# Routing chunks of nine and nine tiles, and the softplus per attention unit on GpSimd

## The chip, the cores and the metric

One core of a Trainium2 chip runs the whole program. The metric is the device time of one execution in microseconds. Engines are called by the profile's names: PE (matmul) with PEld (its weight load), DVE (VectorE), ACT (ScalarE), POOL (GpSimd) and SP (which issues most DMAs). Each engine works through its own list of instructions in the order in which they were emitted; where a source needs another engine's result it waits at the head of that list.

## The reference, cut to what matters

The program is a chain of three stages over 2304 tokens of width 512: a packed attention, a mixture of eight experts with two experts a token, and a SiLU layer.

```python
logits = x @ w_gate
noise_scale = np.log1p(np.exp(x @ w_noise))          # softplus
noisy_logits = logits + noise_scale * noise
top2 = np.argpartition(-noisy_logits, 2, axis=1)[:, :2]
...
for e in range(E):
    for k in range(2):
        mask = top2[:, k] == e
        h = np.maximum(x[mask] @ w1[e], 0.0)
        out[mask] += top2_w[mask, k, None] * (h @ w2[e])
```

The change touches the softplus and the sorting of tokens to experts.

## The kernel before, in words

**Attention.** The tokens are 18 tiles of 128 rows. Eight packing units (`packed`, one for a batch and half of the heads) make small packed keys and values; ten unpacking units (`unpacked`, numbered 0 to 9, of one or two tiles: 0 to 3 hold tiles 0 to 7, 4 holds tile 8, 5 to 8 hold tiles 9 to 16, 9 holds tile 17) turn them into the tokens' rows. A unit's DVE steps are L398 (maximum), L400 (subtract), L402 (sum), L403, L404 and L405 (scale), with ACT's exponential L401 between L400 and L402. PE then transposes (`a2p`, L410) and multiplies (`xp`, L419, once for each half `g` of the width); the 16 routing logits of a tile come out beside the row, are collected by DVE in `lg` (L423 for the first half, L421 for the second), ACT copies the row into `xr`, and SP writes it to `xs` in DRAM (L426). There are two `xr` buffers.

**Routing.** `route` runs on a chunk of tiles: before on tiles 0 to 10 (chunk 0, `EARLY` = 11) and on 11 to 17 (chunk 1). It makes softplus out of ACT's exponential and logarithm for large arguments and a polynomial for small ones (L437 to L449, thirteen DVE instructions), the noisy logits (L451, L452), the two best experts (L456, L458), ranks within each expert (`rk`, PE with L471 and L473), and by one-hot products (L486, L488, L493, then PE's `ip`, L500) the list of token rows for each expert, `idx0` after chunk 0 (L503: the first two tiles' worth of expert 0) and `idx` after chunk 1 (L513). `few` and L620 to L622 give the count that decides the branch to a general path, which isn't taken here.

**Expert 0 ahead of the branch.** With `idx0`, POOL gathers two tiles of rows by indirect DMA (L155), PE transposes them (L145, `tps`), and the first block of expert 0 runs (`expert_block`, L167 to L169 and L177 to L179). While it runs, chunk 1 is routed; with `idx` POOL gathers five more tiles, which PE transposes between the block's last matmuls. PE's last transposes end this part, then all engines branch to `routed`, which holds the rest of the program.

**Order.** The units and routing steps are emitted by a slot loop: `START1` and `START2` give each unit's first slot, `LAG1` and `LAG2` its later phases; from slot 9 on, three steps of `route` for chunk 0 are emitted a slot (`RSTEP`). The framework then sets each engine's list by its own estimate of times. POOL also holds eight weight splits (`split`, L112, tensors `wa0l` to `wa7l`) and the copies into `ppBD` (L355) behind each packing unit's `px` (L350).

Of the kernel before, what the change touches and what calls it, by code (L numbers as in the profile page):

```python
# [7 lines left out]
F32 = mybir.dt.float32  # L8
# [11 lines left out]
P = 128  # L20
B, H, S, D, PK = 4, 8, 576, 64, 32
N, DM, E, F, FF = 2304, 512, 8, 1024, 2048
# [8 lines left out]
START2 = (3, 4, 5, 5, 6, 6, 8, 11, 12, 12)  # L31
SWITCH = 12
WLOAD = 4
RSTEP = 3
LAG2 = (0, 1, 3, 3)
BLOCKS = [(0, 2), (2, 4), (6, 4), (10, 4), (14, 4)]
BW = 512
TA, TB = 2, 3
EARLY = 11
LAG = 1  # L40
DELAY = 2

# [2 lines left out]
def body(ctx: ExitStack, tc: tile.TileContext, q, k, v, p, wg, wn, noise, w1, w2, w_in, w_out, out):  # L45
# [171 lines left out]
    with ExitStack() as ax:  # L217
# [147 lines left out]
            cp(A, bd[:, 256:272], wp)  # L365
            yield

        def unpacked(t, n, lg):

            pr, r = divmod(t, 9)  # L370
            qT = sb.tile([P, 8, P], F32, name="qT")
# [42 lines left out]
            for i in range(n):  # L414
                xr = sb.tile([P, 2, 256], F32, name="xr")
                for g in range(2):
                    xp = pMx.tile([P, 272], F32, name="xp", tag="m")
                    for b, sl in parts:
                        T.matmul(xp[sl], aT[:, 2 * i + g, sl], ppBD[b, g], start=True, stop=True)  # L419
                    if g:  # L420
                        V.tensor_tensor(lg[:, i, :], xp[:, 256:272], lg[:, i, :], op=OP.add)  # L421
                    else:
                        V.tensor_copy(lg[:, i, :], xp[:, 256:272])  # L423
                    cp(A, xr[:, g, :], xp[:, 0:256])
                r0 = (t + i) * P
                nc.sync.dma_start(xs[r0:r0 + P, :], xr.rearrange("p a b -> p (a b)"))  # L426
            yield

        def route(t0, n, lg):

            def tl(shape, nm, dt=F32):
                return rt.tile([P, n, *shape], dt, name=f"rt_{nm}{n}", tag=f"rt_{nm}", bufs=1)


            z = lg[:, :, 8:16]
            w, h, sp, sa, big = tl([E], "w"), tl([E], "h"), tl([E], "sp"), tl([E], "sa"), tl([E], "big", I32)
            V.tensor_tensor(w, z, z, op=OP.mult)  # L437
            V.tensor_scalar(sa, z, 20.0, None, op0=OP.min)
            A.activation(sa, sa, AF.Exp)
            A.activation(sa, sa, AF.Ln, bias=1.0)  # L440
            V.tensor_scalar(h, w, 31.0 / 14515200, -17.0 / 645120, op0=OP.mult, op1=OP.add)
            V.tensor_scalar(sp, z, 0.5, 0.6931471805599453, op0=OP.mult, op1=OP.add)
            V.tensor_tensor(h, h, w, op=OP.mult)
            V.tensor_scalar(big, w, 0.25, None, op0=OP.is_gt)
            for c in (1.0 / 2880, -1.0 / 192, 0.125):
                V.scalar_tensor_tensor(h, h, c, w, op0=OP.add, op1=OP.mult)
            V.tensor_tensor(sp, sp, h, op=OP.add)
            V.tensor_tensor(sa, sa, z, op=OP.max)
            V.copy_predicated(sp, big, sa)  # L449
            ny = tl([E], "ny")  # L450
            V.tensor_tensor(ny, sp, nzt[:, t0:t0 + n, :], op=OP.mult)  # L451
# [49 lines left out]
            if t0 + n < NT:  # L501
                V.tensor_tensor(idx_f, idx_f, ip, op=OP.add)
                V.tensor_scalar(idx0, idx_f[:, 0:TA], 0.0, float((t0 + n) * P - 1), op0=OP.max, op1=OP.min)  # L503
                sn = rt.tile([P, E], F32, name=f"sn{n}")
                V.tensor_reduce(sn, ob.rearrange("p n e -> p e n"), axis=AX.X, op=OP.add)
                V.tensor_tensor(seen, seen, sn, op=OP.add)
                V.tensor_copy(seen_b, seen)
                c = pMx.tile([P, E], F32, name="c", tag="m")
                T.matmul(c, ones, seen_b, start=True, stop=True)
                V.tensor_scalar(few, c, float(TA * P), float(N), op0=OP.is_lt, op1=OP.mult)  # L510
            else:
                V.tensor_tensor(idx_f, idx_f, ip, op=OP.add)
                V.tensor_scalar(idx, idx_f, 0.0, float(N - 1), op0=OP.max, op1=OP.min)  # L513
                sn = rt.tile([P, E], F32, name=f"sn{n}")
                V.tensor_reduce(sn, ob.rearrange("p n e -> p e n"), axis=AX.X, op=OP.add)
                V.tensor_tensor(seen_b, seen, sn, op=OP.add)
# [17 lines left out]

        chunks = {0: EARLY, EARLY: NT - EARLY}
        lgs = {t: one.tile([P, n, 16], F32, name=f"lg{t}") for t, n in chunks.items()}
        units1 = [(b, g) for b in range(B) for g in range(2)]
        units2 = [(0, 2), (2, 2), (4, 2), (6, 2), (8, 1), (9, 2), (11, 2), (13, 2), (15, 2), (17, 1)]
        run1, run2 = {}, {}
# [6 lines left out]
        def make2(i):  # L546
            t, n = units2[i]
            t0 = max(c for c in chunks if c <= t)
            return unpacked(t, n, lgs[t0][:, t - t0:t - t0 + n, :])

        def slot_steps(slot):
            for ph in (3, 2, 1, 0):
# [14 lines left out]
        for slot in range(START2[-1] + LAG2[-1] + 1):  # L567
# [23 lines left out]
            for i, s0 in enumerate(START1):  # L591
                if slot == s0 + WLOAD:
# [2 lines left out]
                        load_w1(W[0], 0, i, G)  # L595
                    else:
                        load_w2(W[0], 0, i - 4, G)
            if slot >= START2[5] + LAG2[3]:
                run(r0, RSTEP)
        for _ in r0:  # L600
            pass
        tick()
        tick()
        r1 = route(EARLY, NT - EARLY, lgs[EARLY])
# [297 lines left out]
```

## Time and profile before

| quantity | us |
|---|---|
| median of 3 runs | 1019.39 (1017.34 to 1020.85) |
| profiled execution, time | 1018.89 |
| profiled execution, span | 1016.9 |
| PE busy | 974.1 (96%) |
| DVE busy | 436.3 (43%) |
| ACT busy | 348.0 (34%) |
| POOL busy | 208.6 (21%) |

All times below are from the span's start. The profiled execution lies 0.5 us under the median. PE is busy for nearly all of the span; the stretch in which it isn't is the one before 161.55 us, where the routed part's first matmul stands.

### The profile page before, as it was taken

Reading aid. Unit: us, or ns where it says so; the run is one execution under the profiler, and the core shown is the slowest. Engines: PE = TensorE matmul, PEld = TensorE weight load, DVE = VectorE, ACT = ScalarE, POOL = GpSimd, SP = SyncE. Lnnn points to the kernel's source line nnn. Section 1 sums busy time; section 2 is a strip of 40 time slices with the busy share of each in tenths; the row PEclk is TensorE's granted clock in tenths of the full one; section 3 lists DMA queues with packets and bytes.
Section 4 is the critical chain, followed back from the end, with each engine's and each line's share of the span. In section 5 each row is a group of like instructions: output and inputs, shape, how many; then the busy total and the mean of one; then the engine's idle time right before and its main releaser. Section 6 shows DMA issues by size and latency. Waiting matters only on the chain.

```text
span 1016.9 us, 14321 instructions
## 1 busy us (share of the span) xinstructions
PE 974.1 (96%) x5672; PEld 836.5 (82%) x5672; DVE 436.3 (43%) x843; ACT 348.0 (34%) x631; POOL 208.6 (21%) x221
## 2 busy tenths in 40 slices
PE   6988796999999999999999998999999999999997
PEld 3776686899999989899999987888888888888885
DVE  3556762565656566575634356422212221111111
ACT  3575321443433334343423254222222222222221
POOL 2162011010101001010100116533323322222221
PEclk9988798999999999999999999999999999999999
DMA  9992224575766656575632436210111101001001
GB/s 247 242 279 90 81 65 137 169 245 147 239 180 210 199 186 219 175 223 181 217 105 93 138 124 204 73 42 22 42 42 32 32 14 39 1 1 42 1 0 42
DMA packets 80473, 122.48 MB, mean 120 GB/s; under 512 B 14608, under 2 KB 47376, under 8 KB 80400
## 3 DMA queue, kind: packets, MB, share of 16 engines
q1 hardware_dynamic: 74320, 101.57, 32.3%
q0 software_dynamic: 6080, 19.93, 6.5%
q8 instruction: 47, 0.77, 0.3%
q14 instruction: 26, 0.21, 0.1%
HBM read 93.17 MB, written 28.31 MB: 119 GB/s over the span
## 4 chain that ended last, share of the span: by engine, by line
PE 87%; DMA 4%; issue 3%; DVE 2%; SPq 2%; ACT 1%; POOL 1%; POOLq 0%; ACTq 0%; DVEq 0%
PE hps L167 13%; PE hps L169 13%; PE hps L168 13%; PE acc L178 13%; PE acc L177 13%; PE acc L179 13%; PE tps L145 2%; PE xp L419 2%; PE s L388 1%; DMA vm<-in_v_dram 1%; SPq L236 1%; DMA ys<-ysb 1%; DMA kr<-in_k_dram 1%; PE s L321 1%; DMA y<-ys,slots 1%
## 5 line engine op out<-in xcount | busy, mean ns | idle before, releaser
L702 POOL TENSOR_TENSOR gl<-sg,gh 128x512 fp32r<-128x512 f32 (+1 forms) x80 | 95.3, 1193 | 252.4 <-ACT gh L701 237.0
L190 ACT ACTIVATE hh<-hps 128x384 fp32r<-128x384 f32 (+1 forms) x128 | 56.1, 438 | 261.7 <-PE hps L169 249.6
L698 DVE TENSOR_TENSOR sg<-hps,sg 128x512 f32<-128x512 f32 (+1 forms) x80 | 50.7, 635 | 195.6 <-ACT sg L697 195.2
L191 DVE SCALAR_TENSOR_TENSOR hl<-hps,hh 128x384 fp32r<-128x384 f32 (+1 forms) x128 | 62.8, 490 | 149.5 <-ACT hh L190 147.5
L155 POOL DMA_INDIRECT xg<-xs,idx x40 | 42.9, 1072 | 355.2 <-PE tps L145 302.7
L697 ACT ACTIVATE sg<-hps 128x512 f32<-128x512 f32 (+1 forms) x80 | 44.4, 555 | 189.0 <-PE hps L169 186.0
L701 ACT ACTIVATE gh<-sg 128x512 fp32r<-128x512 f32 (+1 forms) x80 | 47.1, 589 | 82.3 <-DVE sg L698 82.1
L688 POOL DMA_INDIRECT y<-ys,slots x36 | 37.9, 1053 | 120.5 <-DMA ys<-ysb 82.9
L148 DVE TENSOR_TENSOR xla<-tps,xha 128x512 fp32r<-128x512 f32 x26 | 17.9, 690 | 30.0 <-ACT xha L147 29.9
L419 PE MATMUL xp<-ppBD,a2T 128*128 128x272 f32 (+1 forms) x80 | 26.4, 471 | 2.5 <-ACT xr L51 2.2
L148 DVE TENSOR_TENSOR xlb<-tps,xhb 128x512 fp32r<-128x512 f32 x32 | 22.0, 687 | 15.0 <-ACT xhb L147 14.9
L692 DVE SCALAR_TENSOR_TENSOR y<-y,gates,y 128x512 f32<-128x512 f32 x18 | 14.3, 796 | 28.9 <-DMA y<-ys,slots 28.8
L147 ACT ACTIVATE xhb<-tps 128x512 fp32r<-128x512 f32 x32 | 19.1, 597 | 19.1 <-PE tps L145 19.1
L691 DVE TENSOR_SCALAR y<-y,gates 128x512 f32<-128x512 f32 x18 | 9.2, 512 | 38.2 <-DMA y<-ys,slots 38.2
L167 PE MATMUL hps<-xhb,wa0h 128*128 128x384 f32 (+1 forms) x48 | 17.6, 367 | 7.8 <-issue 7.8
L145 PEld LDWEIGHTS tps<-ident,xg 128*128 128x128 f32 x160 | 19.7, 140 | 5.6 <-ACT xha L147 0.4
L145 PE MATMUL tps<-ident,xg 128*128 128x128 f32 x160 | 23.9, 272 | 0.2
L641 DVE SCALAR_TENSOR_TENSOR t<-raw,t 128x512 int32<-128x512 int32 x32 | 22.2, 693 | 1.1
L642 DVE SCALAR_TENSOR_TENSOR t<-raw,t 128x512 int32<-128x512 int32 x32 | 22.1, 690 | 0.9
L147 ACT ACTIVATE xha<-tps 128x512 fp32r<-128x512 f32 x26 | 15.5, 596 | 19.7 <-PE tps L145 19.7
L638 ACT ACTIVATE t<-raw 128x512 f32<-128x512 f32 x32 | 21.0, 658 | 0.0
L167 PE MATMUL hps<-xha,wa3h 128*128 128x256 f32 (+1 forms) x56 | 17.7, 316 | 3.2 <-DVE sg L698 3.2
(438 smaller groups left out, 2959.1 us busy)
## 6 DMA issues: line engine op xcount, KB each, us to landing
raw<-in_moe_w_dram SPq DMA_DIRECT2D x64, 512.0 KB, 4.0
ys<-ysb SPq DMA_DIRECT2D x40, 256.0 KB, 2.7
raw<-in_moe_w_in_dram SPq DMA_DIRECT2D x16, 512.0 KB, 4.2
raw<-in_moe_w_out_dram SPq DMA_DIRECT2D x16, 512.0 KB, 3.5
xs<-xr SPq DMA_DIRECT2D x18, 256.0 KB, 2.1
km<-in_k_dram SPq DMA_DIRECT2D x8, 512.0 KB, 7.6
vm<-in_v_dram SPq DMA_DIRECT2D x8, 512.0 KB, 7.7
qm<-in_q_dram SPq DMA_DIRECT2D x8, 512.0 KB, 8.2
```

The costliest lines, as they stand in the source:

```text
L145: pin(T.transpose(ps[:, c, :], src[:, c * P:(c + 1) * P], ident))
L167: T.matmul(ps, wh[:, c, s], xh[:, c, :n], start=c == 0, stop=False)
L168: T.matmul(ps, wh[:, c, s], xl[:, c, :n], start=False, stop=False)
L169: T.matmul(ps, wl[:, c, s], xh[:, c, :n], start=False, stop=c == 3)
L177: T.matmul(y, hh[:, s], wh[:, f % 2, :], start=f == 0, stop=False)
L178: T.matmul(y, hh[:, s], wl[:, f % 2, :], start=False, stop=False)
L179: T.matmul(y, hl[:, s], wh[:, f % 2, :], start=False, stop=f == last)
L190: A.activation(hh, ps, AF.Relu)
L191: V.scalar_tensor_tensor(hl, ps, 0.0, hh.bitcast(F32), op0=OP.max, op1=OP.subtract)
L698: V.tensor_tensor(sg, ps, sg, op=OP.mult)
L701: A.activation(gh, sg, AF.Copy)
L702: G.tensor_tensor(gl, sg, gh.bitcast(F32), op=OP.subtract)
```

## The change

Chunk 0 has nine tiles, so chunk 1 has nine too. The softplus leaves `route`: each unpacking unit calls `softplus` for its own one or two tiles as soon as their logits are there. Thirteen instructions a unit go to POOL (ten of them one behind another), two to ACT, and the last maximum to DVE; `route` begins with the predicated copy. What is left of chunk 0's `route` is emitted whole in slot 9. `few` is set to zero at the start and computed for expert 0 alone.

```diff
-RSTEP = 3
-EARLY = 11
+EARLY = 9
+        def softplus(c0, i, n, lg):
+            sp, sa, big = (x[:, i:i + n, :] for x in soft[c0])
+            z = lg[:, i:i + n, 8:16]
+            w, h = (sb.tile([P, n, E], F32, name=f"sp{c}{n}", tag=f"sp{c}") for c in "wh")
+            G.tensor_tensor(w, z, z, op=OP.mult)
+            G.tensor_scalar(sa, z, 20.0, None, op0=OP.min)
+            A.activation(sa, sa, AF.Exp)
+            A.activation(sa, sa, AF.Ln, bias=1.0)
+            G.tensor_scalar(h, w, 31.0 / 14515200, -17.0 / 645120, op0=OP.mult, op1=OP.add)
+            G.tensor_scalar(sp, z, 0.5, 0.6931471805599453, op0=OP.mult, op1=OP.add)
+            G.tensor_tensor(h, h, w, op=OP.mult)
+            G.tensor_scalar(big, w, 0.25, None, op0=OP.is_gt)
+            for c in (1.0 / 2880, -1.0 / 192, 0.125):
+                G.tensor_scalar(h, h, c, None, op0=OP.add)
+                G.tensor_tensor(h, h, w, op=OP.mult)
+            G.tensor_tensor(sp, sp, h, op=OP.add)
+            V.tensor_tensor(sa, sa, z, op=OP.max)
...
-            for c in (1.0 / 2880, -1.0 / 192, 0.125):
-                V.scalar_tensor_tensor(h, h, c, w, op0=OP.add, op1=OP.mult)
-            V.tensor_tensor(sp, sp, h, op=OP.add)
-            V.tensor_tensor(sa, sa, z, op=OP.max)
+            sp, sa, big = soft[t0]
             V.copy_predicated(sp, big, sa)
...
-                V.tensor_scalar(few, c, float(TA * P), float(N), op0=OP.is_lt, op1=OP.mult)
+                V.tensor_scalar(few[:, 0:1], c[:, 0:1], float(TA * P), float(N), op0=OP.is_lt, op1=OP.mult)
...
-            if slot >= START2[5] + LAG2[3]:
-                run(r0, RSTEP)
-        for _ in r0:
-            pass
+            if slot == START2[4] + LAG2[3]:
+                for _ in r0:
+                    pass
```

Three places in the engines' lists show what moves. First DVE around `idx0`, before (the lines are those of the old kernel; `mx_1607` and `sd_1551` belong to units 8 and 7):

```order
L525 SCALAR_TENSOR_TENSOR rt_rr_1582<-chosen,rt_rr_1582 128x22
L405 TENSOR_TENSOR sd_1551<-sd_1551,mx_1549 128x512
L493 TENSOR_TENSOR rt_oa_1426<-iota_lo,rt_lo_1370 128x768 x3
L493 TENSOR_TENSOR rt_oa_1426<-iota_lo,rt_lo_1370 128x512
L400 TENSOR_TENSOR sd_1609<-s_1598,mx_1607 128x512
L526 SCALAR_TENSOR_TENSOR slots<-rt_rr_1582,rt_up_1584 128x22
L510 TENSOR_SCALAR few<-c 128x8
L502 TENSOR_TENSOR idx_f<-idx_f,ip 128x40
L503 TENSOR_SCALAR idx_103<-idx_f 128x2
L402 TENSOR_REDUCE mx_1607<-sd_1609 128x16
```

Units 7 and 8 stand between the steps of chunk 0. And now, in the changed kernel (its lines 500 to 510 are the old 493 to 503; `mx_1669` is unit 7):

```order
L532 SCALAR_TENSOR_TENSOR rt_rr_1501<-chosen,rt_rr_1501 128x18
L500 TENSOR_TENSOR rt_oa_1466<-iota_lo,rt_lo_1461 128x768 x3
L533 SCALAR_TENSOR_TENSOR slots<-rt_rr_1501,rt_up_1503 128x18
L517 TENSOR_SCALAR few<-c 128x1
L509 TENSOR_TENSOR idx_f<-idx_f,ip 128x40
L510 TENSOR_SCALAR idx_103<-idx_f 128x2
L350 TENSOR_SCALAR px<-pp,mx 128x128
L423 COPY lg_198<-xp 128x16
L421 TENSOR_TENSOR lg_198<-xp,lg_198 128x16
L398 TENSOR_REDUCE mx_1669<-s_1660 128x16
```

Chunk 0 runs through without a unit's step, and the last packing unit's `px` and all of units 7 to 9 stand behind `idx0`.

Second PE, from the second-last packing unit's `tp` on, before (`tp`, `wp` and `s_1540` lead to unit 7's scores; the `pp` here is the last packing unit's product):

```order
L357 MATMUL tp<-ident,px 128x128
L347 MATMUL pp<-vm,a1T 32x64 x16
L347 MATMUL pp<-vr,a1T 32x64 x4
L363 MATMUL wp<-wgn,ppT_190 32x16 x4
L388 MATMUL s_1540<-ppT_190,qT 128x2x32 x4
```

Now, directly behind the last of eighteen matmuls into `ip`:

```order
L507 MATMUL ip<-rt_oc_1467,rt_oa_1466 128x40
L347 MATMUL pp<-vm,a1T 32x64 x16
L347 MATMUL pp<-vr,a1T 32x64 x4
L419 MATMUL xp<-ppBD_181,a2T_1573 128x272
L357 MATMUL tp<-ident,px 128x128
L419 MATMUL xp<-ppBD_185,a2T_1573 128x272
L363 MATMUL wp<-wgn,ppT_195 32x16 x4
L388 MATMUL s_1660<-ppT_195,qT 128x2x32 x4
```

The last packing unit's product moved from ahead of chunk 0's ranks to behind chunk 0's whole list.

Third POOL between the gathers of `idx0` and of `idx`, before:

```order
L355 COPY ppBD_192<-px 32x64 x4
L155 DMA xg<-xs,idx_103 128x512 x2
L155 DMA xg<-xs,idx 128x512 x5
L622 TENSOR_LOAD most
```

Now the softplus of units 6 to 9 stands there; its first instructions from tile 17 on (`spw_1849` is unit 9, `sph_1820` unit 8):

```order
L436 TENSOR_TENSOR spw_1849<-lg_198 128x8
L437 TENSOR_SCALAR sa_203<-lg_198 128x8
L441 TENSOR_SCALAR sp_202<-lg_198 128x8
L446 TENSOR_TENSOR sph_1820<-sph_1820,spw_1819 128x16
L440 TENSOR_SCALAR sph_1850<-spw_1849 128x8
L443 TENSOR_SCALAR big_204<-spw_1849 128x8
L445 TENSOR_SCALAR sph_1820<-sph_1820 128x16
L442 TENSOR_TENSOR sph_1850<-sph_1850,spw_1849 128x8
```

From that first row to the last softplus instruction there are nineteen on POOL, and the five gathers with `idx` stand behind them.

## Rows read from the trace of the kernel before

**Rows 1.** The page, chain that ended last, share of the span by engine.
```profile
PE 87%; DMA 4%; issue 3%; DVE 2%; SPq 2%; ACT 1%; POOL 1%; POOLq 0%; ACTq 0%; DVEq 0%
```

**Rows 2.** Stretches: length, busy PE, PEld, DVE, ACT, POOL, granted PE clock, DMA, GB/s.
```profile
100.00:125.00 25.00, 19.61 (x125) 14.85 (x124) 19.00 (x67) 9.56 (x24) 2.81 (x6) 0.66 0.20 65
125.00:150.00 25.00, 24.82 (x173) 19.90 (x173) 15.22 (x78) 5.74 (x15) 4.74 (x5) 1.00 0.25 77
```

**Rows 3.** Timeline, chunk 1 to the branch: start, length, instruction, idle before and releaser.
```profile
128.03 0.16 DVE L421 TENSOR_TENSOR lg<-xp,lg 128x16 f32<-128x16 f32 x1
...
131.42 0.22 DVE L452 TENSOR_TENSOR rt_ny<-rt_ny,lg 128x56 f32<-128x56 f32 x1
131.67 0.58 DVE L456 MAX8 rt_m<-rt_ny 128x8 f32<-128x8 f32 x7
...
138.48 2.16 DVE L493 TENSOR_TENSOR rt_oa<-iota_lo,rt_lo 128x768 f16<-128x768 f16 x3
...
142.16 0.18 DVE L513 TENSOR_SCALAR idx<-idx_f 128x40 int32<-128x40 f32 x1
...
146.81 1.40 PE L145 MATMUL tps<-ident,xg 128*128 128x128 f32 x8
...
153.13 0.60 PE L145 MATMUL tps<-ident,xg 128*128 128x128 f32 x4
...
161.55 0.48 PE L167 MATMUL hps<-xhb,wa0h 128*128 128x384 f32 x1 [7.82 <-issue]
```

**Rows 4.** Timeline of DVE, chunk 0 and units 5 to 9.
```profile
91.61 0.17 DVE L421 TENSOR_TENSOR lg<-xp,lg 128x16 f32<-128x16 f32 x1 [0.28 <-PE xp L419]
...
96.97 0.25 DVE L452 TENSOR_TENSOR rt_ny<-rt_ny,lg 128x88 f32<-128x88 f32 x1
...
97.77 0.35 DVE L350 TENSOR_SCALAR px<-pp,mx 128x128 f32<-128x128 f32 x1 [0.55 <-PE pp L347]
...
103.06 0.69 DVE L398 TENSOR_REDUCE mx<-s 128x16 f32<-128x512 f32 x1 [0.95 <-PE s L388]
...
111.54 3.29 DVE L493 TENSOR_TENSOR rt_oa<-iota_lo,rt_lo 128x768 f16<-128x768 f16 x4
...
115.73 0.17 DVE L503 TENSOR_SCALAR idx<-idx_f 128x2 int32<-128x2 f32 x1
...
117.72 0.68 DVE L405 TENSOR_TENSOR sd<-sd,mx 128x512 f32<-128x512 f32 x1
...
119.55 0.43 DVE L405 TENSOR_TENSOR sd<-sd,mx 128x256 f32<-128x256 f32 x1
```

**Rows 5.** Timeline, tile 15's products and a row copy that waits.
```profile
121.41 1.08 PE L419 MATMUL xp<-ppBD,a2T 128*128 128x272 f32 x4
...
126.66 0.38 ACT L51 ACTIVATE xr<-xp 128x256 f32<-128x256 f32 x1 [0.96 <-DMA xs<-xr]
```

**Rows 6.** POOL's groups by shape: count | busy us, mean ns | idle before, releasers.
```profile
L702 POOL TENSOR_TENSOR gl<-sg,gh 128x512 fp32r<-128x512 f32 x64 | 82.7, 1292 | 226.0 <-ACT gh L701 210.9 <-PE acc L179 14.2
...
L355 POOL COPY ppBD<-px 32x64 f32<-32x64 f32 x32 | 7.8, 245 | 39.1 <-DVE px L350 23.1 <-DVE mx L328 7.6 <-DVE mx L332 7.3
L702 POOL TENSOR_TENSOR gl<-sg,gh 128x256 fp32r<-128x256 f32 x16 | 12.7, 799 | 26.4 <-ACT gh L701 26.2
...
L86 POOL IOTA rowv<- 128x18 f32 x1 | 0.2, 157 | 0.0
```

**Rows 7.** DVE's groups by shape, 50 to 160 us.
```profile
L458 DVE FIND_INDEX8 rt_i<-rt_m,rt_ny 128x8 uint32<-128x8 f32 x18 | 2.5, 161 | 0.0
...
L486 DVE TENSOR_TENSOR rt_oc<-iota_hi,rt_hi 128x880 f16<-128x880 f32 x1 | 1.1, 1066 | 0.0
```

**Rows 8.** Timeline, a weight split on POOL beside a DVE maximum.
```profile
93.20 2.34 POOL L112 TENSOR_TENSOR wa6l<-raw,wa6h 128x1024 fp32r<-128x1024 f32 x1 [16.50 <-ACT rt_sa L440]
...
93.26 2.39 DVE L448 TENSOR_TENSOR rt_sa<-rt_sa,lg 128x88 f32<-128x88 f32 x1
```

**Rows 9.** Stretch of 2 us, columns as in rows 2.
```profile
96.00:98.00 2.00, 2.00 (x50) 1.50 (x51) 1.31 (x6) 0.61 (x3) 1.40 (x5) 0.58 0.00 0
```

More of the change, by code (lines that the diff above doesn't have):

```diff
@@ L98, in body @@
     few = const.tile([P, E], F32)
+    V.memset(few, 0.0)
     M = {"pin": False, "w": 384, "hb": 3}
@@ L366, in packed, with unpacked @@
             yield
-        def unpacked(t, n, lg):
+        def unpacked(t, n, lg, done):
             pr, r = divmod(t, 9)
@@ L426, in unpacked @@
                 nc.sync.dma_start(xs[r0:r0 + P, :], xr.rearrange("p a b -> p (a b)"))
+            done()
             yield
+        def softplus(c0, i, n, lg):
[15 more added lines that the diff above has]
+            V.tensor_tensor(sa, sa, z, op=OP.max)
         def route(t0, n, lg):
@@ L432, in tl @@
                 return rt.tile([P, n, *shape], dt, name=f"rt_{nm}{n}", tag=f"rt_{nm}", bufs=1)
[L435 to L444, printed above, removed]
-            for c in (1.0 / 2880, -1.0 / 192, 0.125):
-                V.scalar_tensor_tensor(h, h, c, w, op0=OP.add, op1=OP.mult)
-            V.tensor_tensor(sp, sp, h, op=OP.add)
-            V.tensor_tensor(sa, sa, z, op=OP.max)
+            sp, sa, big = soft[t0]
             V.copy_predicated(sp, big, sa)
@@ L536, in body @@
         lgs = {t: one.tile([P, n, 16], F32, name=f"lg{t}") for t, n in chunks.items()}
+        soft = {t: [one.tile([P, n, E], dt, name=f"{c}{t}") for c, dt in (("sp", F32), ("sa", F32), ("big", I32))]
+                for t, n in chunks.items()}
         units1 = [(b, g) for b in range(B) for g in range(2)]
@@ L548, in make2 @@
             t0 = max(c for c in chunks if c <= t)
-            return unpacked(t, n, lgs[t0][:, t - t0:t - t0 + n, :])
+            return unpacked(t, n, lgs[t0][:, t - t0:t - t0 + n, :], lambda: softplus(t0, t - t0, n, lgs[t0]))
         def slot_steps(slot):
```

## The prediction

> **What bounds the kernel now.** I read the chain that ended last first: PE has 87% of it [rows 1]. Then the stretches: from 100 to 125 us PE is busy for 19.61 of 25 us and its granted clock is 0.66 of full, from 125 to 150 us it is busy for 24.82 [rows 2]; from 161.55 us on, where the branch body's first matmul stands [rows 3], PE hardly waits again. So the changed part can move the end only by moving the moment at which PE leaves for the branch, and everything behind it shifts as a block.
>
> That moment is PE's last transposes of gathered rows: 153.13 + 0.60 = 153.73 us [rows 3]. Followed back, it hangs on chunk 1. Tile 17's last logits are ready at 128.03 + 0.16 = 128.19; the noisy logits at 131.42 + 0.22 = 131.64, **3.45 us** later; `idx` at 142.16 + 0.18 = 142.34, **10.70 us** later; the first transposes of rows gathered with it start at 146.81, **4.47 us** later, and **6.92 us** of PE work follow to 153.73 [rows 3]. PE is busy all the while with expert 0's first block, but it reaches the transposes just as the rows land, so a later `idx` is a later end.
>
> **The change part by part.** I walk the changed lists along the same chain.
>
> *Chunk 0.* Its nine tiles don't start when tile 8 is ready: on POOL the last softplus step of unit 4 stands behind the first two of unit 5, and on DVE the predicated copy stands behind tile 10's logits. So it starts after 91.61 + 0.17 = 91.78 [rows 4], as before. Four more small ACT instructions of some 0.2 us lie on the way of those logits; I take 0.5 us. Three POOL steps of 0.21 us (priced below) follow: the copy starts at about 93.0. Before, the noisy logits were done at 96.97 + 0.25 = 97.22 [rows 4], with a stall of over 2 us inside [rows 8]; now at about 93.8. From there to `idx` chunk 1 took 10.70 us for seven tiles with other work between [rows 3]; two more tiles cost 1.45 (below), and three DVE steps of the expert block, which chunk 0 doesn't have, fall away: 10.8 us. Two weight splits of 2.34 us still stand on POOL in this time, and one held a DVE instruction for 2.39 us [rows 8]; I allow 1.5 of a possible 2.3. `idx0` is then ready at 93.8 + 10.8 + 1.5 = **106.1** instead of 115.73 + 0.17 = 115.90 [rows 4].
>
> *Units 7 to 9.* The gain of 9.8 us isn't kept, because these units' DVE steps stood between chunk 0's and now stand behind them, and so does the last packing unit. From its `px` at 97.77 to unit 7's first step at 103.06 took 5.3 us [rows 4], of which 1.8 were PE work that is now done earlier; with 1.1 us for its `pp` ahead, unit 7 starts 4.6 us after `idx0`, at **110.7** instead of 103.06. From there DVE has only the units: unit 7 takes 0.7 + 0.7 + 0.65 (ACT) + 0.7 + 0.4 + 0.7 and gaps, some 4.1 us; unit 8 another 6.1 to the end of its last step, since unit 9 and tile 13's logits stand within it. That is 120.9 against 117.72 + 0.68 = 118.40 before, and unit 9 ends at 122.3 against 119.55 + 0.43 = 119.98 [rows 4]: later by over 2 us. Some of that comes back: tile 14 and the first gathered rows no longer stand ahead of tile 15 on PE, so tile 15's products come 1.5 us behind unit 8 (transposes, ACT copy), at 122.4 instead of 121.41 [rows 5]. From there to tile 17's logits took 128.19 - 121.41 = 6.8 us, with a row copy that waited 0.96 us for a DMA write [rows 5]; a DVE step of 0.69 no longer stands within, so 6.2. Tile 17's logits: **128.6**, or +0.4. Bounds: -2.0 without the allowance for the splits and with `idx0` 0.5 earlier, +4 if POOL steps cost their upper bound and both splits hold DVE.
>
> *The softplus of unit 9 on POOL.* Behind tile 17's logits nineteen POOL instructions are left, against DVE's thirteen before that were done within the 3.45 us. The trace has no POOL arithmetic of this size. Nearest are a copy of 64 elements at 245 ns and an iota of 18 at 157 [rows 6]; from the two shapes of the subtraction, 1292 ns for 512 and 799 for 256 elements, a line through both gives 306 ns at none [rows 6]. So 0.10 to 0.34 us each, and I take 0.21, between copy and iota: 4.0 us. Then copy, two tensor operations and one step of the expert block, 1.15: the noisy logits come 5.2 us behind the logits instead of 3.45, **+1.75** (from -0.35 to +4.2).
>
> [...]
>
> *Two more tiles in chunk 1.* Index search of 0.161 us [rows 7] and maximum of 0.58 / 7 [rows 3] per tile, overlapped to about 0.21: 0.42. Two products over 40 elements a tile: 1066 / 11 = 97 ns [rows 7], twice, for two tiles: 0.39. The third piece of the row one-hots has three tiles instead of one: before 2.16 us for seven tiles [rows 3], 3.29 for eleven [rows 4], so 0.28 a tile, 0.56. Small ones 0.1. Together **+1.45**.
>
> *PE's list.* The ranks of chunk 1 (`rk`) stand one quarter of a block later on PE than before, and PE comes to them a little after DVE is ready: **+0.5** (0 to 0.7).
>
> *The rest.* DVE loses some 2.9 us of softplus in each chunk; in chunk 0 the walk above has it, in chunk 1 it is the 3.45. The single-column count and the memset cost nothing: the count is ready before `idx`, and what hides it is the gathers. The two queues that the gathers of `idx0` now share with softplus steps don't matter, since PE takes those rows only behind tile 16. The list of SP is the same, but three of its row writes stand behind weight loads that wait for POOL's splits; these have slack if a POOL step stays under 0.35 us.
>
> *Sum:* 0.4 + 1.75 + 1.45 + 0.5 = +4.1 us on the profiled execution's 1018.89, that is 1023.0. The median lies 0.5 above that execution, so on the scale of the runs 1023.0 to 1023.5: **1023.2**.
>
> **The rivals.** *A: POOL steps are cheap and the splits miss DVE.* At 0.12 us the nineteen take 2.3 us (+0.05), and tile 17's logits come 1.5 earlier: the sum is about +0.5, 1019.9. For it: POOL's iota and the overlap of units 8 and 9. Against: each polynomial step waits for the one before.
>
> *B: faster.* Chunk 0's earlier index pulls the whole attention tail: if PE runs at its full clock from 104 us on and no split holds DVE, `idx0` comes at 104.1, unit 7 starts at 107.9, units 7 to 9 end 2.8 earlier than in my walk, and if tile 17's row copy doesn't wait for a write, its logits come at 122.5. With softplus at 4.5 and 12.15 to `idx` that is 139.15, 3.2 before the old one: 1016.0. It decides once tile 17's logits are ready before about 123. [...]
>
> *C: POOL holds DVE.* A maximum of 0.2 us on DVE took 2.39 because it began just behind a split on POOL [rows 8]. Now over fifty small POOL steps run beside the routing. If both splits and a good part of the steps hold chunk 0's products, and PE falls to half clock while it waits for `ip` within the block, 2 us come on top of the upper half of the terms: +9.5, 1028.5.
>
> [...]
>
> *D: the nine tiles are nine in name only* is not a rival but part of the walk, since chunk 0 waits for tile 10 anyway.
>
> **How the numbers follow.** The forecast's case has 0.50 and spans 1020.5 to 1026; A 0.25; C 0.13; B 0.12. A measurement of this kernel can tell about 0.3%, 3.1 us: from 1016.3 to 1022.4 is no change. Of the forecast's half some 0.12 lie below 1022.4, so: faster 0.12, same 0.25 + 0.12 = 0.37, slower 0.51. Range: 1017.3 leaves out most of B, 1029 leaves out the end of C.
>
> **What would show it.** Right: `idx0` near 106 us, unit 7's first maximum near 110, tile 17's logits near 128.6, noisy logits 5 us behind them with DVE waiting for POOL, `idx` near 146.5, the branch body near 165.6. Wrong: POOL's softplus steps at a pitch under 0.15 us; tile 17's logits before 126; or PE waiting for something else than gathered rows ahead of the branch. The time behind the branch body's first matmul must not change; if it does, the whole argument is off.

## The result, and the profile after

The changed kernel's median is 1025.36 us (1020.08 to 1029.42) against 1018.85 us (1013.82 to 1020.85) for the kernel before, measured together: a ratio of 1.0067, with a 95% interval from 1.0043 to 1.0092. Two later sets on other occasions gave 1.0049 (1.0032 to 1.0066) and 1.0062 (1.0037 to 1.0087). The medians differ by 6.5, 4.4 and 7.3 us.

The profiled execution is the fastest of its set: 1020.08 us, span 1018.1 us. Its stretches, in the view of [rows 2] (length, then busy time of PE, PE's weight loads, DVE, ACT and POOL; the last three numbers are the granted clock, the share of the DMA engines and GB/s):

```profile
core 0: us, PE busy (x) PEld busy (x) DVE busy (x) ACT busy (x) POOL busy (x), PEclk, DMA share, GB/s
75.00:100.00 25.00, 16.64 (x165) 12.13 (x165) 16.88 (x90) 13.48 (x40) 18.36 (x65) 0.84 0.19 74
100.00:125.00 25.00, 20.26 (x165) 14.38 (x163) 13.84 (x44) 10.63 (x30) 13.52 (x42) 0.82 0.25 85
125.00:150.00 25.00, 22.18 (x148) 18.19 (x148) 13.01 (x68) 3.64 (x12) 8.53 (x23) 0.93 0.16 48
```

From 125 to 150 us PE was busy for 24.82 us before [rows 2]; now for 22.18, and from 75 to 100 us it stands idle for 8.4 of 25 us. DVE's steps of chunk 0, answering to [rows 4], are: tile 10's last logits, the copy that begins the noisy logits, `idx0`, the last packing unit's `px`, and unit 7's first step:

```profile
start us, us, engine line op out<-in xcount [idle before <-releaser]
88.36 0.17 DVE L421 TENSOR_TENSOR lg<-xp,lg 128x16 f32<-128x16 f32 x1 [0.28 <-PE xp L419]
90.60 0.24 DVE L456 COPY_PREDICATED sp<-big,sa 128x72 f32<-128x72 int32 x1 [2.07 <-POOL sp L447]
102.05 0.17 DVE L510 TENSOR_SCALAR idx<-idx_f 128x2 int32<-128x2 f32 x1
103.22 0.35 DVE L350 TENSOR_SCALAR px<-pp,mx 128x128 f32<-128x128 f32 x1 [1.01 <-PE pp L347]
106.81 0.69 DVE L398 TENSOR_REDUCE mx<-s 128x16 f32<-128x512 f32 x1 [1.11 <-PE s L388]
```

And chunk 1's, answering to [rows 3]: tile 17's last logits, the copy, the end of the noisy logits, the last piece of the row one-hots, `idx`:

```profile
123.89 0.17 DVE L421 TENSOR_TENSOR lg<-xp,lg 128x16 f32<-128x16 f32 x1
129.62 0.24 DVE L456 COPY_PREDICATED sp<-big,sa 128x72 f32<-128x72 int32 x1 [2.30 <-POOL sp L447]
130.39 0.22 DVE L459 TENSOR_TENSOR rt_ny<-rt_ny,lg 128x72 f32<-128x72 f32 x1
139.91 2.69 DVE L500 TENSOR_TENSOR rt_oa<-iota_lo,rt_lo 128x768 f16<-128x768 f16 x3
143.24 0.18 DVE L520 TENSOR_SCALAR idx<-idx_f 128x40 int32<-128x40 f32 x1
```

Both copies wait more than 2 us for POOL's last softplus step. On PE chunk 0's products now begin with one long wait, chunk 1's have three small ones, and the branch body begins 1.84 us later than in [rows 3]:

```profile
99.66 0.38 PE L507 MATMUL ip<-rt_oc,rt_oa 128*128 128x40 f16 x6 [4.33 <-DVE rt_oa L500]
...
140.92 0.32 PE L507 MATMUL ip<-rt_oc,rt_oa 128*128 128x40 f16 x6 [0.19 <-DVE rt_oa L500]
141.79 0.32 PE L507 MATMUL ip<-rt_oc,rt_oa 128*128 128x40 f16 x6 [0.54 <-DVE rt_oa L500]
142.66 0.32 PE L507 MATMUL ip<-rt_oc,rt_oa 128*128 128x40 f16 x6 [0.55 <-DVE rt_oa L500]
...
149.34 1.03 PE L145 MATMUL tps<-ident,xg 128*128 128x128 f32 x8
155.29 0.60 PE L145 MATMUL tps<-ident,xg 128*128 128x128 f32 x4
163.39 0.69 PE L167 MATMUL hps<-xhb,wa0h 128*128 128x384 f32 x1 [7.50 <-issue]
```

Two things are odd: this execution is only 1.2 us longer than the one profiled before, where the medians differ by 6.5, and tile 10's logits come 3.25 us earlier (88.36 against 91.61 [rows 4]), ahead of most that was changed.

### The profile page after: what moved, and what is told of

Read it like the earlier page. It is cut to its first block, busy times and chain, and to the rows that moved or that the text cites. A ratio compares the mean times of both kernels' runs of the same rounds, so it can differ in the third digit from the quotient of the medians.

```text
span 1018.1 us, 14455 instructions
## 1 busy us (share of the span) xinstructions
PE 972.0 (95%) x5672; PEld 834.6 (82%) x5672; DVE 433.6 (43%) x831; ACT 348.8 (34%) x647; POOL 238.1 (23%) x351
## 4 chain that ended last, share of the span: by engine, by line
PE 85%; DMA 4%; DVE 3%; SPq 2%; issue 2%; POOL 2%; ACT 1%; ACTq 0%; POOLq 0%; DVEq 0%
PE hps L167 13%; PE hps L169 13%; PE hps L168 13%; PE acc L178 13%; PE acc L177 13%; PE acc L179 13%; PE tps L145 2%; DMA y<-ys,slots 2%; PE xp L419 1%; SPq L236 1%; DMA vm<-in_v_dram 1%; PE s L388 1%; DMA km<-in_k_dram 1%; DMA ys<-ysb 1%; DVE y L700 1%
## 5 line engine op out<-in xcount | busy, mean ns | idle before, releaser
L148 DVE TENSOR_TENSOR xlb<-tps,xhb 128x512 fp32r<-128x512 f32 x32 | 21.9, 687 | 15.8 <-ACT xhb L147 15.4
L167 PE MATMUL hps<-xha,wa3h 128*128 128x256 f32 (+1 forms) x56 | 17.7, 316 | 3.0 <-DVE sg L706 3.0
```

Source lines behind the costliest of these rows:

```text
L167: T.matmul(ps, wh[:, c, s], xh[:, c, :n], start=c == 0, stop=False)
```

## The experiments

All ratios are to the kernel before, run on the same chip at the same time. "PE leaves" is the end of PE's last work before the branch body, "idle" is PE's time without work between 50 us and there (the length of that stretch less PE's busy time in it). Both come from one profiled execution a row, the ratio from 6 to 12 executions. The first column names the kernel.

| kernel | chunks | emission of chunk 0 | softplus | ratio (95%) | PE leaves, us | idle, us |
|---|---|---|---|---|---|---|
| before | 11+7 | stepped | whole chunk, DVE | 1 | 153.73 | 12.85 |
| before, again | 11+7 | stepped | whole chunk, DVE | 0.9987 (0.9963–1.0010) | 152.23 | 12.64 |
| nine tiles alone | 9+9 | stepped | whole chunk, DVE | 1.0007 (0.9984–1.0030) | 153.63 | 14.07 |
| without POOL | 9+9 | one point | whole chunk, DVE | 1.0015 (0.9989–1.0041) | 155.38 | 14.41 |
| POOL for chunk 1 | 9+9 | one point | chunk 0 DVE, chunk 1 POOL | 1.0027 (1.0004–1.0050) | 157.45 | 14.45 |
| one point alone | 11+7 | one point | whole chunk, DVE | 1.0047 (1.0026–1.0068) | 158.28 | 16.83 |
| **changed** | 9+9 | one point | per unit, POOL | 1.0067 (1.0043–1.0092) | 155.89 | 17.53 |
| changed, again | 9+9 | one point | per unit, POOL | 1.0049 (1.0032–1.0066) | 157.04 | 21.27 |
| changed, third | 9+9 | one point | per unit, POOL | 1.0062 (1.0037–1.0087) | 160.73 | 16.65 |
| POOL for chunk 0 | 9+9 | one point | chunk 0 POOL, chunk 1 DVE | 1.0056 (1.0032–1.0080) | 160.57 | 19.58 |
| last units on DVE | 9+9 | one point | POOL, units 8 and 9 DVE | 1.0066 (1.0043–1.0089) | 157.78 | 17.31 |
| per unit on DVE | 9+9 | one point | per unit, DVE | 1.0038 (1.0023–1.0053) | 166.23 | 21.91 |
| eleven tiles | 11+7 | one point | per unit, POOL | 1.0096 (1.0067–1.0125) | 163.84 | 25.90 |
| POOL alone | 11+7 | stepped | per unit, POOL | 1.0101 (1.0076–1.0126) | 161.37 | 21.83 |

The three rows of the changed kernel show how far the idle column can be trusted: 16.65 to 21.27 us in one kernel, and the execution with the least left last, since PE was busy for longer there at a lower clock: 94.08 us at a mean granted clock of 0.85, against 88.36 at 0.89 and 85.77 at 0.92. Rows that differ by 2 or 3 us in it aren't told apart by it.

### Both kernels once more

No edit. First the changed kernel:

> The changed kernel as it is, for a second profiled execution. In the first one tile 10's last logits were ready at 88.36 us, 3.25 us earlier than in the kernel before (91.61), though the change has nothing ahead of the loads that moved there; the branch body began at 163.39, which is 75.0 us behind those logits instead of 69.9. Theory 1: the early front was luck of the loads, so the front is not tied to the change; counted from tile 10's logits the branch body comes 75 us (74 to 77) later in every execution, and the median stays 5 to 7 us above the kernel before (1023.5 to 1026). Theory 2: the front is earlier because of the change, and what the other executions lose against the first lies elsewhere, in stretches of half clock between 140 and 165 us: then tile 10's logits come at about 88.4 again, and the distance to the branch body is over 77 us.

It gave 1023.09 us (ratio 1.0049), with tile 10's logits at 89.75 us and the second matmul of the branch body at 164.86, 75.1 us behind them. Then the kernel before:

> The kernel before as it is, for a second profiled execution and for what two sets of runs of one kernel differ by. Theory 1: tile 10's logits come anywhere between 88 and 92 us, with the wait for the loads of the shared expert's keys and values; counted from there the branch body comes after 69 to 71 us; the ratio to the kernel before is 1.000 within 0.003. Theory 2: the logits come at 91.6 again, since the front belongs to the kernel.

It gave 1018.61 us (ratio 0.9987), tile 10's logits at 89.64 and the second matmul at 161.28, 71.6 us behind. A third execution of the changed kernel came later, beside the run with the last units on DVE:

> The changed kernel as it is, a third profiled execution beside the run above. Theory 1: from tile 10's logits to the second matmul of the branch body 74 to 76 us, as in the first two (75.5 and 75.1), against 70.1 and 71.6 in the kernel before, whatever the time of tile 10's logits; median 4 to 6.5 us above the kernel before. Theory 2: the first two profiled executions, each the fastest of its set, are not like the others: 77 us or more, with more half clock between 90 and 160 us.

It gave 1024.30 us, ratio 1.0062. Tile 10's logits, `idx`, PE's last transposes and the branch body of that execution:

```profile
92.12 0.17 DVE L421 TENSOR_TENSOR lg<-xp,lg 128x16 f32<-128x16 f32 x1 [0.28 <-PE xp L419]
...
149.34 0.18 DVE L520 TENSOR_SCALAR idx<-idx_f 128x40 int32<-128x40 f32 x1
...
160.13 0.60 PE L145 MATMUL tps<-ident,xg 128*128 128x128 f32 x4
168.09 0.69 PE L167 MATMUL hps<-xhb,wa0h 128*128 128x384 f32 x1 [7.36 <-issue]
```

So tile 10's logits are ready at 88.5, 89.8 and 92.3 us in the changed kernel, and at 91.8 and 89.6 in the kernel before: where they stand isn't tied to the kernel. Counted from there PE leaves after 67.4, 67.3 and 68.4 us, against 62.0 and 62.6. This is the change's cost, some 5.4 us, and the profiled execution hid 3.25 us of it by an early front. So theory 1 holds in its main point and theory 2 falls, with misses at the edges: to the second matmul of the branch body the changed kernel takes 75.4, 75.1 and 76.3 us (74 to 76 expected of the third), the kernel before 71.6 in its second execution (69 to 71 expected), and the medians lie 4.4 us (5 to 7 expected) and 7.3 us (4 to 6.5 expected) above the kernel before.

### The parts one by one

Nine tiles alone (before, with one number changed):

```diff
-EARLY = 11
+EARLY = 9
```

> The kernel before with chunks of nine and nine tiles and nothing else changed. Theory 1: chunk 1's noisy logits to its index takes 12.8 us instead of 10.7 as measured in the changed kernel, chunk 0's index comes some 2 us earlier and units 7 to 9 keep a part of that: 0 to 2 us slower than the kernel before. Theory 2: the size is the whole loss of the changed kernel: 4 to 6 us slower.

1019.41 us, ratio 1.0007: theory 1, no difference. The profile shows a gain and a loss of the kind expected: tile 17's logits come 34.0 us behind tile 10's instead of 36.4, and the way from noisy logits to `idx` takes 12.4 us instead of 10.7.

One point alone (before, eleven tiles):

```diff
-            if slot >= START2[5] + LAG2[3]:
-                run(r0, RSTEP)
-        for _ in r0:
-            pass
+            if slot == START2[5] + LAG2[3]:
+                for _ in r0:
+                    pass
```

> The kernel before with the routing of chunk 0 emitted at one point (where its first steps stand now); eleven tiles, softplus in one piece on DVE. Theory 1: noisy logits at 95 us, idx0 at 107 instead of 115.9, units 7 to 9 behind it and 1 to 2 us later than before, tile 17's logits 1 to 2 us later, chunk 1 as before: 0 to 3 us slower than the kernel before. Theory 2: one point is what the change gains by, because chunk 0 is done in one piece and DVE has only the units behind it: 1 to 3 us faster.

1024.59 us, ratio 1.0047, more than theory 1 allowed. `idx0` came at 108.79 us, but `idx` only 1.3 us later than in the kernel before (143.60), so the index chain alone doesn't explain 4.8 us. PE's timeline shows what else happened; these are its waits in chunk 0:

```profile
95.81 0.33 PE L356 MATMUL tp<-ident,px 128*128 128x128 f32 x1 [2.50 <-DVE px L349]
...
100.38 0.23 PE L470 MATMUL rk<-rt_ob,before 128*128 128x88 bf16 x1 [1.33 <-DVE rt_ob L464]
105.70 0.38 PE L499 MATMUL ip<-rt_oc,rt_oa 128*128 128x40 f16 x6 [4.70 <-DVE rt_oa L492]
```

With everything of chunk 0 in one piece PE's list has its products `ip` ahead of the work of units 7 to 9, and PE stands for 4.70 us until DVE has made the one-hots.

POOL alone (before with the changed kernel's `softplus`, called at the end of each unit; chunks and stepping as before):

> The kernel before with the softplus per unit on POOL alone; chunks of eleven and seven tiles, and three steps of the routing a slot, as before. Theory 1: chunk 1's noisy logits come 6.5 us behind tile 17's logits instead of 3.45, +3.1; chunk 0's on DVE are 2.9 us shorter, so units 7 to 9 come up to 2 us earlier; together 1 to 3 us slower than the kernel before. Theory 2: the softplus on POOL costs nothing by itself, within 1 us of the kernel before or faster.

1028.29 us, ratio 1.0101: far worse than theory 1. POOL's weight splits and the last softplus step of tiles 9 and 10 in this kernel:

```profile
95.94 2.36 POOL L112 TENSOR_TENSOR wa6l<-raw,wa6h 128x1024 fp32r<-128x1024 f32 x1
...
99.84 2.35 POOL L112 TENSOR_TENSOR wa7l<-raw,wa7h 128x1024 fp32r<-128x1024 f32 x1
...
105.28 0.22 POOL L447 TENSOR_TENSOR sp<-sp,sph 128x16 f32<-128x16 f32 x1
```

Chunk 0 of eleven tiles needs unit 5's softplus, and that stands on POOL behind two splits and eight copies: its last step begins 12.5 us behind tile 10's logits, and chunk 0's copy starts at 105.54 instead of 96.39. The third experiment of the kind takes the changed kernel and undoes the size alone:

```diff
-EARLY = 9
+EARLY = 11
```

> The changed kernel with chunks of eleven and seven tiles again; softplus per unit on POOL and the single point stay. Theory 1: chunk 0 now needs unit 5's softplus too, whose sixteen steps stand on POOL around the two weight splits of 2.35 us; in the run with POOL's softplus alone its last step came 12.5 us behind tile 10's logits. So chunk 0's copy comes 6 us or more later than in the changed kernel (97 us or later), everything of units 7 to 9 follows it, and the 2.1 us that two tiles fewer save in chunk 1 don't make up for it: 3 to 6 us slower than the changed kernel. Theory 2: the size is a cost by itself, two tiles in chunk 1 are late work: 1 to 2 us faster than the changed kernel.

1029.01 us, ratio 1.0096: theory 1 in size and place. The copy of chunk 0 waits 6.08 us for POOL:

```profile
90.42 0.17 DVE L421 TENSOR_TENSOR lg<-xp,lg 128x16 f32<-128x16 f32 x1 [0.28 <-PE xp L419]
99.37 0.26 DVE L456 COPY_PREDICATED sp<-big,sa 128x88 f32<-128x88 int32 x1 [6.08 <-POOL sp L447]
```

So nine tiles are worth nothing in the order of the kernel before, but some 3 to 5 us (1.0096 against 1.0049 to 1.0067) once chunk 0 is emitted at one point and POOL makes the softplus, since unit 4's is done before the first split begins (its last step ends at 90.56 us in the changed kernel, the split begins at 91.66). The three parts don't add.

### Where POOL's softplus costs

The changed kernel with the softplus of the kernel before (over a whole chunk in `route`, eleven steps on DVE and two on ACT; what is called thirteen DVE steps elsewhere counts ACT's two):

> The changed kernel's chunks of nine and one point of emission, with the softplus as in the kernel before: thirteen steps over the whole chunk on DVE. What is left of the change without POOL. Theory 1: the noisy logits of chunk 1 come 3.5 us behind tile 17's logits instead of 6.55 (3 us gained), those of chunk 0 come at 94 to 95 us instead of 91.4 and take units 7 to 9 with them (2 to 3 us lost on the way to tile 17's logits): within 2 us of the changed kernel, and slower than the kernel before by 3 to 5. Theory 2: POOL's softplus is the loss, in price and in what it holds: 4 us or more faster than the changed kernel, at or below the kernel before.

1020.07 us, ratio 1.0015, which lies between the theories: 3.5 to 5.3 us below the changed kernel, and not told apart from the kernel before. It is also 4.5 us below one point alone (1024.59 us, run together; the means differ by 3.9 with an interval of 1.3 to 6.6), so with chunk 0 at one point nine tiles help without POOL too: PE's first wait for `ip` is 2.40 us instead of 4.70. `softplus` on DVE for each unit (every `G.` in it a `V.`):

> The changed kernel with the softplus steps of each unit on DVE instead of POOL (sixteen instructions a unit, the same ones); all else as changed. Theory 1: POOL's price of 0.26 to 0.30 us a step is what the last unit costs: noisy logits 3.3 us behind tile 17's logits instead of 6.55, about 3.2 us gained there; units 5 to 8 put some 50 steps of 0.1 to 0.2 us on DVE between their own, so tile 17's logits come 1 to 2 us later; together 1 to 2.5 us faster than the changed kernel. Theory 2: the softplus on POOL is covered and the loss is in the order and the chunk size: within 1 us of the changed kernel, or slower by the 1 to 2 us on DVE.

1023.07 us, ratio 1.0038, the same as the changed kernel within the intervals, so theory 2. But that is no proof that POOL is harmless, since DVE lost time of its own. Two of unit 1's steps, which take 0.17 us elsewhere, took 2.3 us each beside two weight splits that POOL began at 72.42 and 74.75 us, and tile 10's logits came only at 97.7 us (88.5 to 93.0 us in the profiled executions of the other kernels):

```profile
72.53 2.30 DVE L442 TENSOR_TENSOR sph<-sph,spw 128x16 f32<-128x16 f32 x1
74.86 2.27 DVE L445 TENSOR_SCALAR sph<-sph 128x16 f32<-128x16 f32 x1
```

The test of my own account was to shorten what POOL has to do behind tile 17's logits, and nothing else:

```diff
+            U = V if c0 + i >= 15 else G
...
-            G.tensor_tensor(w, z, z, op=OP.mult)
+            U.tensor_tensor(w, z, z, op=OP.mult)
...
+                if U is V:
+                    V.scalar_tensor_tensor(h, h, c, w, op0=OP.add, op1=OP.mult)
```

> The changed kernel with the softplus of units 8 and 9 alone (tiles 15 to 17) on DVE, thirteen steps a unit; units 0 to 7 keep theirs on POOL. In two executions of the changed kernel the noisy logits came 6.55 and 6.59 us behind tile 17's logits, in the kernel before 3.45 twice. Theory 1: the POOL steps behind tile 17's logits are the part of POOL's softplus that costs: noisy logits 3 to 3.7 us behind tile 17's logits, chunk 0 as in the changed kernel (its copy 2 us behind tile 10's logits), so 2.5 to 3.5 us faster than the changed kernel and within 3 us of the kernel before. Theory 2: what POOL costs is what its steps hold on DVE and PE on the way (chunk 0, units 5 to 7): within 1 us of the changed kernel although the noisy logits come earlier.

1023.06 us, ratio 1.0066, against 1.0062 for the changed kernel run together: no gain. The noisy logits did come earlier, 3.99 us behind tile 17's logits instead of 6.55, and `idx` at 142.13, which is 52.9 us behind tile 10's logits instead of 54.9 to 57.2. PE still left 68.6 us behind tile 10's logits (67.3 to 68.4 in the changed kernel). From the end of `idx`'s products (141.69 us) on PE waits for nothing that the view shows, and it still needs 16.1 us, some of it at the lower clock (0.76 from 141 to 144 and 0.67 from 144 to 147). The clock alone isn't why nothing was gained: from tile 10's logits to PE's leaving its mean is 0.80 here and in the third execution of the changed kernel, which took 68.4 us.

```profile
139.63 0.32 PE L511 MATMUL ip<-rt_oc,rt_oa 128*128 128x40 f16 x6
140.50 0.32 PE L511 MATMUL ip<-rt_oc,rt_oa 128*128 128x40 f16 x6 [0.54 <-DVE rt_oa L504]
141.37 0.32 PE L511 MATMUL ip<-rt_oc,rt_oa 128*128 128x40 f16 x6 [0.55 <-DVE rt_oa L504]
...
148.07 1.39 PE L145 MATMUL tps<-ident,xg 128*128 128x128 f32 x8
...
152.11 1.03 PE L145 MATMUL tps<-ident,xg 128*128 128x128 f32 x8
...
155.80 0.60 PE L145 MATMUL tps<-ident,xg 128*128 128x128 f32 x4
...
157.16 0.63 PE L179 MATMUL acc<-wa7h,hl 128*128 128x512 f32 x2
164.44 0.69 PE L167 MATMUL hps<-xhb,wa0h 128*128 128x384 f32 x1 [6.66 <-issue]
```

The gathers were no longer late; PE was. A part of the block (twelve matmuls with `wa2h` and `wa2l`, two with `wa5h`, four with `wa6h` and `wa6l`, some 3.3 us) stands ahead of these products in the changed kernel and behind them here, so the edit also moved PE's list; but whether PE does that part before or after, it has the same work to do before it can leave. That made a third theory: PE has a fixed amount of work up to the branch, so what it once stood idle, or ran at the lower clock, it doesn't win back, wherever `idx` stands. Two kernels tested where POOL's share of the idle time arises. POOL for chunk 0 alone (chunk 1 in one piece on DVE):

```diff
+            if c0 != 0:
+                return
...
+            if t0 != 0:
+                z = lg[:, :, 8:16]
...
```

> The changed kernel with POOL's softplus for chunk 0 alone; chunk 1's in one piece of thirteen steps on DVE, as in the kernel before. Counted from 50 us to PE's last transposes, PE was idle for 12.6 and 12.8 us in the kernel before, for 16.7, 17.5 and 21.3 in three executions of the changed one, 17.3 with the last units on DVE and 14.4 without POOL's softplus. Theory 3 (after the last units' run): the end is set by PE's idle time on the way, and POOL costs where chunk 0's copy waits 2.1 us for POOL behind tile 10's logits: its products come 13.7 us behind these instead of 12.0, and PE waits 4.3 us for them instead of 2.4. Then this kernel is like the changed one: 1.0040 to 1.0065 of the kernel before, idle 16.5 us or more. Theory 1 (chunk 1's tail on POOL is the cost): like the kernel without POOL's softplus, 1.0000 to 1.0030.

1023.50 us, ratio 1.0056, idle 19.58 us: in the ranges of theory 3, above that of theory 1. One thing in it is not in the changed kernel, though: the copy of chunk 0 took 2.36 us instead of 0.24, just behind a split that POOL began at 94.51, so `idx0` came 15.6 us behind tile 10's logits instead of the 13.7 expected, and this adds to its loss.

```profile
94.59 2.36 DVE L473 COPY_PREDICATED sp<-big,sa 128x72 f32<-128x72 int32 x1 [1.57 <-POOL sp L449]
```

And the opposite, POOL for chunk 1 alone (the same edit with the two conditions reversed):

> The changed kernel with POOL's softplus for chunk 1 alone; chunk 0's in one piece on DVE, begun when tile 8's logits are ready. Theory 3: chunk 0's products come 12 us behind tile 10's logits, PE waits 2.4 us for them, and the later noisy logits of chunk 1 (6.55 us behind tile 17's) cost 1 us or less, because PE has the block's work to do meanwhile: 1.0005 to 1.0030 of the kernel before, idle 14 to 15.5 us. Theory 1: chunk 1's tail costs 3 us: 1.0040 to 1.0065.

1021.38 us, ratio 1.0027, idle 14.45 us: within theory 3's range, below theory 1's, although the noisy logits of chunk 1 come 5.88 us behind tile 17's logits. PE's first wait for `ip` was 1.78 us (2.4 expected). The intervals of this ratio and of the one with POOL for chunk 0 overlap (1.0004 to 1.0050 and 1.0032 to 1.0080), while the two kernels set against each other, run together, differ by 2.7 us in the mean (0.6 to 4.9). With the held copy in the first of them, the split of POOL's cost between the chunks is likely, not proven; that chunk 1's tail alone isn't the cost has two runs behind it.

In the runs with nine tiles and one point, chunk 0's products are the place: `idx0` comes 13.7 us behind tile 10's logits in all three executions of the changed kernel and 12.0 us without POOL's softplus, because the copy waits for POOL's last step instead of starting with tile 8. PE's first wait for `ip` is then 4.33 and 4.34 us (changed kernel) against 2.40:

```profile
100.56 0.38 PE L499 MATMUL ip<-rt_oc,rt_oa 128*128 128x40 f16 x6 [2.40 <-DVE rt_oa L492]
```

## Why the prediction was right, and where its reasons were not

The forecast was slower, 1023.2 us, and 1025.36 (1023.09 and 1024.30 in the later sets) lies in its range. Step by step, counted from tile 10's logits where the front moves all times:

| step | predicted | measured in three executions |
|---|---|---|
| `idx0` behind tile 10's logits | 106.1 − 91.78 = 14.3 | 13.7, 13.75, 13.7 |
| unit 7's first maximum behind `idx0` | 4.6 | 4.6, 4.3, 5.4 |
| unit 8 ends behind `idx0` | 14.8 | 15.4, 16.1, 17.5 |
| unit 9 ends behind `idx0` | 16.2 | 16.7, 17.7, 19.0 |
| tile 17's logits against before | +0.4 | −1.3, −0.3, +1.0 |
| softplus of unit 9 | +1.75 | +3.1, +3.1, +3.1 |
| noisy logits to `idx` | +1.95 | +2.1, +2.15, +2.1 |
| from `idx` to PE's leaving | 0 | +1.2, 0, −0.1 |
| PE leaves, behind tile 10's logits | +4.1 | +5.1, +5.0, +6.2 |

(Tile 17's row and the last two are measured against the mean of the two executions of the kernel before: 36.8, 11.3 and 62.3 us.) The *walk through chunk 0 and units 7 to 9* was right to within 0.6 us in the first execution, but 1.3 to 2.8 us short at units 8 and 9 in the others, and tile 17's logits scatter by over 2 us. Its `idx0` was met partly by luck: the copy began 2.07 us behind tile 10's logits instead of 1.2, and the 1.5 us allowed for the splits weren't needed. The price of *two more tiles* with the `rk` term was right to within 0.2 us.

**The softplus of unit 9** was mis-sized: 6.55 us from logits to noisy logits, not 5.2. POOL, still at two steps of unit 8, starts unit 9's 0.59 us behind tile 17's logits, for which the sum had nothing. The nineteen steps then take 4.93 us instead of 4.0, from 124.65 to 129.58, 0.26 each as two units' chains interleave; where unit 9's chain runs alone, its steps start 0.32 and 0.28 us apart (the last three rows). These are rows of the first execution:

```profile
124.65 0.20 POOL L436 TENSOR_TENSOR spw<-lg 128x8 f32<-128x8 f32 x1
124.93 0.24 POOL L437 TENSOR_SCALAR sa<-lg 128x8 f32<-128x8 f32 x1
...
128.78 0.24 POOL L445 TENSOR_SCALAR sph<-sph 128x8 f32<-128x8 f32 x1
129.10 0.20 POOL L446 TENSOR_TENSOR sph<-sph,spw 128x8 f32<-128x8 f32 x1
129.38 0.20 POOL L447 TENSOR_TENSOR sp<-sp,sph 128x8 f32<-128x8 f32 x1
```

A row's own time, 0.20 to 0.25 us, is what I assumed for the whole step; the 0.08 us from its end to the next start was left out. No run shows the 0.10 us a step at the low end of the prediction's range, nor rival A's 0.12; the nineteen steps took 0.26 us each, so rival A is gone.

**The chain of reasons** failed at the first step, "a later `idx` is a later end". The prediction took the chain through chunk 1 for the only thing that sets PE's leaving, because PE reached the transposes just as the rows landed [rows 3]. The other side was as tight: from 125 to 150 us PE had 24.82 us of work in 25 [rows 2]. So an earlier `idx` brings nothing by itself: the last units' run took 2.6 us off the noisy logits and PE left no earlier. The loss of 5 to 6 us is better told as PE's idle time between tile 10's logits and PE's leaving (columns as in [rows 2]; the kernel before twice, then the changed kernel's three executions):

```profile
91.78:153.73 61.95, 53.88 (x427) 42.53 (x424) 43.66 (x193) 19.21 (x50) 13.31 (x17) 0.83 0.21 66
89.64:152.23 62.59, 55.03 (x427) 43.66 (x424) 43.70 (x193) 19.18 (x50) 13.30 (x17) 0.81 0.20 65
88.53:155.89 67.36, 53.21 (x427) 41.63 (x424) 39.34 (x175) 19.46 (x56) 30.61 (x88) 0.85 0.19 61
89.75:157.04 67.29, 52.34 (x427) 39.82 (x424) 39.55 (x175) 19.48 (x56) 30.78 (x88) 0.87 0.19 61
92.29:160.73 68.44, 56.39 (x427) 43.87 (x424) 39.71 (x175) 19.69 (x56) 30.62 (x88) 0.80 0.18 60
```

PE has the same 427 matmuls to do and is busy for much the same time, longer where the clock is lower. It is idle for 8.07 and 7.56 us before and for 14.15, 14.95 and 12.05 us after: 5.9 us more in the mean, where PE leaves 5.4 us later. In the view of PE's waits over these stretches (us in total, times, longest) the matmuls `ip` stand out; the first line is the kernel before, the second the changed kernel, and the other executions of each agree:

```profile
PE ip L500 <- DVE rt_oa L493: 1.1, 3, 0.5
PE ip L507 <- DVE rt_oa L500: 6.6, 6, 4.3
```

That is 5.5 us more, and what else changed nearly cancels: less waiting for DVE's `px` and `sd`, more for ACT. The same wait is 3.8 us with POOL for chunk 1, 4.5 without POOL, and 6.3 to 6.4 with one point alone, with POOL for chunk 0 and with the last units on DVE, so the kernels under 1.003 all have less of it. It doesn't give the size, though: POOL alone has 4.7 at a ratio of 1.0101. The prediction gave it no term; rival C names PE's wait for `ip`, but only together with the half clock. Its own sign of being wrong, PE waiting for something else than gathered rows ahead of the branch, came true in all three executions, and another, tile 17's logits before 126 us, in the first. That the sum of the terms met the measured value is partly chance: the late `idx` and PE's late work are two descriptions of the same delay, and the runs show that mending the first alone isn't enough.

**What stood.** Everything behind PE's leaving took 863.2 and 865.2 us before (span less the time at which PE leaves) and 862.2, 861.3 and 862.8 after, and behind the branch body's first matmul 855.3 and 856.4 before and 854.7, 853.9 and 855.4 after; the block shifts as a whole. Rival B (faster by an earlier tail) had its mechanism in one execution: tile 17's logits came at 124.06, near its point of 123, but with the front's help, and the time was not below the old one. (B's 122.5 us doesn't come out of its terms: 2.8 and 0.96 us off 128.6 are 124.8. Nor does A's sum, whose terms give +0.9, not +0.5.) Rival C's hold by POOL showed only in small: a step of chunk 0 took 0.52 us beside the split at 91.66; no split held a product in the changed kernel. The half clock (0.50 granted from 98 to 106 us in the kernel before, and from 94 to 104 in the changed one's first execution) was not the loss either: in the stretches above the mean granted clock is 0.83 and 0.81 before and 0.85, 0.87 and 0.80 after, and the mean of whole executions is 0.977, 0.981 and 0.980 in three sets of the changed kernel and 0.977 to 0.980 in sets of the kernel before.

What stays open: the exact split of the 5 to 6 us between the one point and POOL in the changed kernel, since the parts don't add (0.15% for nine tiles and one point together, 0.35 to 0.5% more with POOL, on intervals of 0.2% either way). The count for expert 0 alone and the memset were not tried by themselves. No version here beats the kernel before: nine tiles alone is level with it.

## What to carry to other kernels

When an engine's list is full up to a branch, count its idle time up to there first, and ask of each edit what it adds to that; a chain that ends just in time can be one of two equal limits, and shortening it alone gave nothing here. Emitting a long chain on one engine at one point put the partner engine's dependent instructions together as well: PE stood for 4.70 us (one point alone) and 4.33 us (changed kernel) ahead of its first `ip` products, where its longest wait for them in the kernel before was 0.5. Work moved to a "free" engine came as late here as what stood ahead of it in that engine's list: with POOL alone unit 5's last step began 12.5 us behind tile 10's logits, behind two splits of 2.36 and 2.35 us and eight copies. Before moving work, look up what stands there, and profile more than one execution when the front of the program moves by more than the effect.

## What the runs showed of the hardware

- Elementwise steps of 8 or 16 elements on POOL took 0.20 to 0.28 us by their rows, with a few exceptions, and one that depends on the one before started 0.28 to 0.34 us behind it; two interleaved chains went at 0.26 us a step.
- Small DVE steps beside a POOL weight split of 2.34 to 2.38 us took 2.27 to 2.36 us instead of 0.17 to 0.24 (per unit on DVE, POOL for chunk 0). Not every step beside a split was longer: the index searches of the changed kernel's chunk 0 (L465, 92.36 to 93.6 us) took 0.15 to 0.16 us each beside the split that POOL began at 91.66. The reverse was seen too: two POOL softplus steps in the changed kernel's first execution took 0.76 and 0.93 us instead of 0.22 beside two DVE products of 0.90 us (`rt_oc`, from 96.63 and 97.64 us).
- Within a set of executions of one kernel the time tends to be longer where the mean granted clock is lower, loosely: in the kernel without POOL's softplus 1014.7 us at 0.983, 1024.9 at 0.974 and at 0.977, but also 1018.7 at 0.977. That is wider than the change's whole effect, and a single profiled execution can stand at either end.
- Between PE's last work and the branch body's first matmul stand 6.7 to 8.8 us in most kernels here, whoever was late before; in two of them (nine tiles alone, POOL alone) one matmul came after 2.3 and 3.5 us, and a second pause of 3.0 and 3.6 us followed. In the kernel per unit on DVE one pause of 3.55 us was all, so that PE's late leaving there (166.23 us) overstates its loss.
